# Two small blocks take each half of the weights together, and the first batch's second-half units follow at once

## Chip, cores and metric

One core of a Trainium2 chip runs the kernel. The metric is device microseconds of one execution. The engines are named as in the profile: PE (TensorE matmuls), PEld (its weight loads), DVE (VectorE), ACT (ScalarE), POOL (GpSimd), SP (SyncE, which issues most DMAs).

## What is computed

Attention with a compressed memory for 4 batches of 8 heads of 576 tokens of 64 numbers, then two feed-forward layers over the 2304 tokens of 512 numbers, with 2048 hidden channels. Everything is fp32, and the weights of both layers arrive as 64-bit floats.

```python
scores = scale * np.matmul(q, k.transpose(0, 1, 3, 2))   # causal mask, softmax -> a
local = np.matmul(a, v)
q_p = phi(q)                                             # max(q, 0) + exp(min(q, 0))
mem_out = np.einsum('bhsd,bhde->bhse', q_p, M_prev) / mem_norm
x = g * mem_out + (1 - g) * local
...
h = x @ w_in                                             # layer 1
g = s * np.maximum(h, 0.0) ** 2 + b
x = g @ w_out
...
g = h * np.tanh(sp)                                      # layer 2, sp = log(1 + exp(h))
y = g @ w_out
```

## The kernel before

The order of the work is written by a planner at build time: every step has an engine, a duration, a priority (`prio`, smaller first) and the steps and buffers that it needs. The planner runs through time with these and gives each engine one fixed list. On the chip each engine goes down its list in order and waits at a row until that row's inputs are there.

**Attention.** A unit is two heads of one batch and either the first three tiles of 128 rows (`TA`, called a first-half unit here) or the last two (`TB`, second-half unit). There are 32 units (`pair`, from L429). Each does its score products on PE (L539), row minima on DVE (L549), exponentials on ACT (L557), sums and reciprocals (L504, L578), a scaling of the rows (L573 on ACT, L575 on DVE or POOL), transposes on PE (L598) with copies on ACT (L603), and a product with the values (L620). Its result goes through `xs` (L635) to `x_d` in memory (L637). In the first batch the scaling of a first-half unit is done by DVE, in later batches by POOL; a second-half unit has one tile scaled by ACT and one by DVE.

The inputs of the first four units lie in the weight buffers of the last quarter (`PLACE`, `STAGED`), the following ones in one buffer each of `qk`, `qn` and `vx`; a second one of each comes when the layer-1 weights are all converted. The order of units is: four first-half units of batch 0, then in turn a second-half unit of one batch and a first-half unit of the next. Their priorities are 7 apart (`STEP`).

**Weights of layer 1.** 32 pieces (`convert`) of 128x512 words, in four quarters: of each quarter (`r`) four pieces of `w_in`, then four of `w_out`. Each costs DVE three rows (L685, L687, L697), ACT two (L683, L694) and POOL one (L679). Their raw words pass through `stage` and through weight buffers that are not yet in use.

**Layer 1.** Tokens in three small blocks of 256 and three of 512. A small block goes through the 16 groups of hidden channels in 8 pairs: for each pair 24 matmuls with `w_in` (L780) into the one bank `h`, then `rt` (ACT L829, DVE L835), `gh` and `gl` (ACT L838, DVE L840), then 24 matmuls with `w_out` (L856) that add up in two banks. Two matmuls with zeros (L852) open those banks for a block. A pair's second product comes two pairs after its first (`LAG1`), and `h` is one bank, so the first product of a pair waits for `rt` of the one before it. Block 0 takes the first 256 tokens straight from the attention (`xh`, `xl`, L632, L633); the other blocks load theirs back from `x_d` (`load_x`, L799 to L801). A block needs all four quarters of the weights one after the other. All this has low priority on PE (500 and up), so it fills PE between the steps of the units. Until the first of it, PE's gaps are filled with products of zeros (L1234).

The three large blocks begin when the attention is over; layer 2 follows.

Of the kernel before, what the change touches and what calls it, by code (L numbers as in the profile page):

```python
# [29 lines left out]
STEP = 7.0  # L30
# [7 lines left out]
PLACE = (0, 1, 2, 3)  # L38
STAGED = 4
# [299 lines left out]
def attention_then_two_ffn(ctx: ExitStack, tc: tile.TileContext, qk, qz, vm, beta,  # L339
# [101 lines left out]
    def pair(b, p, prio, g, place=None, apart=False):  # L441
# [14 lines left out]
        if place is None:  # L456
            qk_b, qn_b, vx_b = (Buf(R[x], [P, n]) for x, n in zip(("qk", "qn", "vx"), sizes))
            starts = 0, 0, 0
        else:
            qk_b = qn_b = vx_b = Buf(R[("wih", "wil", "woh", "wol")[place], NR - 1], [P, sum(sizes)])  # L460
            starts = 0, sizes[0], sizes[0] + sizes[1]
# [52 lines left out]
        if apart:  # L514
            low = [Buf(R["Pt3"], [P, 4 * P]) for _ in range(2)]
            high = [Buf(R["Pt4"], [P, 5 * P]) for _ in range(2)]
            Pt = {(i, t): ((low, 0), (high, 0), (high, 2 * P))[t] for t in g for i in range(2)}
            Pt = {(i, t): (x[i], a) for (i, t), (x, a) in Pt.items()}
        else:
            Pt = {(i, t): (Buf(R[f"Pt{t}"], [P, P * (t + 1)]), 0) for t in g for i in range(2)}  # L520
# [106 lines left out]
        k = 0  # L627
# [7 lines left out]
        add(ACT, act_us(m - k) - 0.04, lambda: nc.scalar.copy(xs.t[:, k:m], pv.t[:, skip + k:n]), [pv], [xs])  # L635
        c0 = b * S + q0
        add(DMA, 0.7, lambda: nc.sync.dma_start(x_d[:, p, c0 + k:c0 + m], xs.t[:, k:m]), [xs], [x_in[b, groups_all.index(g)]])  # L637
# [206 lines left out]
    def y_part(j, fcs, acc, t, gh, gl, gh_bufs, gl_bufs, prio):  # L844
# [4 lines left out]
        def y(part, k, fc):  # L849
            if fc == 0 and part == 0 and not big:  # L850
                for a in acc:
                    nc.tensor.matmul(a.t.rearrange("p (k n) -> p k n", n=P), zeros,  # L852
                                     zeros.unsqueeze(1).to_broadcast([P, 4, P]), start=True, stop=False)
            x, nm = ((gh, "woh"), (gh, "wol"), (gl, "woh"))[part]
            for ec in range(NCC):
                nc.tensor.matmul(acc[ec // per].t[:, (ec % per) * n:(ec % per + 1) * n],  # L856
                                 w_at(nm, fc // FPR, fc % FPR)[:, ec * P:(ec + 1) * P], t(x)[:, k * n:(k + 1) * n],
                                 start=(big and fc == 0 and part == 0),
                                 stop=(fc == NFC - 1 and part == 2 and ec % per == per - 1))

        for part in range(3):
            for k, fc in enumerate(fcs):
                need = [*(gl_bufs if part == 2 else gh_bufs), W["wol" if part == 1 else "woh", fc // FPR]]
                add(PE, 0.48 if not big else 0.908, prio, lambda part=part, k=k, fc=fc: y(part, k, fc),
                    need + (acc if fc or part else []), acc, keep=[gh[0]])

    def y_out(j, acc, prio):

        t0, n = blocks1[j]
# [3 lines left out]
        mine = [y_in[t1 // N1] for t1 in range(t0, t0 + n, N1)]  # L873
        for a in (2, 3, 0, 1) if big else (0, 1):
            place = "xr" if not big else "yr" if j < NB1 - 1 else "xh" if a % 2 else "xl"
            ys, act = Buf(R[place], [P, per, n]), a % 2 == 1

            def evacuate(a=a, act=act, ys=ys):
                (nc.scalar.copy if act else nc.vector.tensor_copy)(ys.t, acc[a].t.rearrange("p (k n) -> p k n", n=n))

            add(ACT if act else DVE, 0.7, prio, evacuate, [acc[a]], [ys])
            add(DMA, 0.002 * n * per, prio, lambda a=a, ys=ys: nc.sync.dma_start(
                y_d[:, a * per:(a + 1) * per, t0:t0 + n], ys.t), [ys], mine)
# [225 lines left out]
    halves_ = [(0, p, TA) for p in range(H // 2)]  # L1109
    for i in range(B * H // 2):  # L1110
        halves_.append((*divmod(i, H // 2), TB))
        if i + H // 2 < B * H // 2:
            halves_.append((*divmod(i + H // 2, H // 2), TA))
    for i, x in enumerate(halves_[:STAGED]):
        pair(x[0], x[1], STEP * i, x[2], PLACE[i % len(PLACE)], i < H // 2 and i % 2 == 1)
# [3 lines left out]
    for i, p in enumerate(pieces):  # L1119
        convert(1, 3.0 * i - 1.0 if i < 4 else 22.0 + 2.0 * (i - 4) if i < 8 else 30.0 + 2.4 * (i - 8), *p, raws[i])  # L1120
# [3 lines left out]
    for i, x in enumerate(halves_[STAGED:]):  # L1124
        pair(x[0], x[1], STEP * (i + STAGED), x[2])

# [5 lines left out]
    seq = [(j, tuple(range(fc, fc + 2 - (j >= NB1 - NBIG)))) for j in range(NB1) for fc in range(0, NFC, 2 - (j >= NB1 - NBIG))]  # L1132

    def rank1(j, fc):
        i = NFC * j + fc
        i += max(0, i - NFC * (NB1 - NBIG))
        return RANK1 + i
# [4 lines left out]
    for i in range(len(seq)):  # L1142
        order1.append((i, True))
        for k in range(n, len(seq)):
            if k + LAG1[seq[k][0] >= NB1 - NBIG] > i and i < len(seq) - 1:
# [3 lines left out]
    for i, begins in order1:  # L1149
        j, fcs = seq[i]  # L1150
        little, m0 = j < NB1 - NBIG, len(plan.steps)
        if begins:
            if fcs[0] == 0:
                if j > 0:
                    load_x(j, -1.0)
                accs[j] = [Buf(R[x], [P, 512]) for x in BANKS[j]]
            at_ = rank1(j, fcs[0])
# [125 lines left out]
```

## Time and profile before

| | us |
|---|---|
| median of three timed runs | 986.79 (985.3 to 987.03) |
| the profiled execution | 990.28 |
| its span, first to last instruction | 988.2 |
| PE busy in the span | 956.4 |

The profiled execution is 3.5 us (0.35%) above the median of the timed runs, and 2.1 us of it lie outside the span. PE's busy time counts the products with zeros, 98 before the first layer-1 product. In the profile a row of a group gives line, engine, operation, output and inputs, count, busy time and mean duration, then the idle time before it and what ended that. The rows quoted below are numbered in groups.

### The profile page before, as it was taken

What the parts mean: (1) busy time and instruction counts of PE and PEld (TensorE: products, weight loads), DVE (VectorE), ACT (ScalarE), POOL (GpSimd) and SP (SyncE); (2) the same over time, 40 slices, a digit from 0 to 9 for tenths busy, and PEclk for the clock granted to TensorE, in tenths of its full rate; (3) what the DMA queues carried; (4) which work ended last, traced back from release to release, by engine and by line L of the source; (5) the groups of instructions that cost most, each with busy time, mean ns of one, the idle gap of its engine ahead of it and who ended that gap; (6) DMA issues with size and microseconds to landing.
All of it is one profiled execution on the core that took longest, in us unless ns stands there. A gap on an engine that the chain in (4) does not pass through costs nothing.

```text
span 988.2 us, 18045 instructions
## 1 busy us (share of the span) xinstructions
PE 956.4 (97%) x6304; PEld 850.5 (86%) x6304; DVE 668.6 (68%) x1614; ACT 637.9 (65%) x1377; POOL 191.3 (19%) x354
## 2 busy tenths in 40 slices
PE   6899888999999999999999999999999999999998
PEld 5678577887878898888888888999999999999998
DVE  6989987765765366688612143489966799567864
ACT  4878768777797668798745566366643466344552
POOL 5536656553552000000000000000010001100100
PEclk9989999999999999999999999999999999999999
DMA  9756465544454179998730134487686666676465
GB/s 233 226 182 198 132 185 161 163 116 111 127 137 120 52 237 279 281 315 271 244 115 1 43 128 160 129 269 268 217 298 225 205 206 225 230 242 201 146 218 176
DMA packets 98730, 184.68 MB, mean 187 GB/s; under 512 B 12880, under 2 KB 73296, under 8 KB 91344
## 3 DMA queue, kind: packets, MB, share of 16 engines
q1 hardware_dynamic: 91152, 132.15, 43.2%
q0 software_dynamic: 7056, 51.38, 15.4%
q8 instruction: 50, 0.82, 0.3%
q14 instruction: 40, 0.33, 0.1%
q10 hardware_dynamic: 432, 0.01, 0.0%
HBM read 141.04 MB, written 42.47 MB: 186 GB/s over the span
## 4 chain that ended last, share of the span: by engine, by line
PE 64%; issue 18%; DMA 1%; POOL 1%; DVE 1%; ACT 1%; SPq 0%; POOLq 0%; DVEq 0%
PE bank L856 19%; PE bank L780 18%; PE bank L986 10%; PE bank L1052 7%; PE bank L620 4%; PE bank L598 4%; PE bank L539 3%; DMA woh<-wi_split_d 1%; DMA xr<-x_d 1%; POOL woh L967 1%; POOL wol L967 0%; ACT Pt L557 0%; POOL woh L946 0%; ACT PT L603 0%; DVE stage L685 0%
## 5 line engine op out<-in xcount | busy, mean ns | idle before, releaser
L1052 PE MATMUL bank<-wol,S 128*128 128x256 f32 x828 | 111.6, 283 | 0.0
L1052 PEld LDWEIGHTS bank<-wol,S 128*128 128x128 f32 x828 | 105.3, 192 | 0.0
L967 POOL DMA_DIRECT2D wol<-wo_split_d x17 | 9.2, 540 | 457.9 <-DMA stage<-wo_d 350.7
L986 PE MATMUL bank<-wi,woh 128*128 128x384 f32 x423 | 97.1, 335 | 0.7 <-DMA woh<-wi_split_d 0.7
L557 ACT ACTIVATE Pt<-Pt,mx 128x64 f32<-128x64 f32 (+4 forms) x160 | 88.7, 562 | 8.5 <-DVE mx L549 7.1
L1052 PE MATMUL bank<-woh,S 128*128 128x256 f32 x684 | 93.1, 283 | 0.0
L1052 PEld LDWEIGHTS bank<-woh,S 128*128 128x128 f32 x684 | 87.1, 192 | 0.0
L603 ACT COPY PT<-bank 128x384 f32<-128x384 f32 (+2 forms) x160 | 67.8, 489 | 28.6 <-PE bank L598 25.5
L598 PE MATMUL bank<-ident,Pt 128*128 128x128 f32 x480 | 68.5, 280 | 10.2 <-DVE Pt L575 5.8
L986 PEld LDWEIGHTS bank<-wi,woh 128*128 128x128 f32 x423 | 75.3, 188 | 1.7 <-DMA woh<-wi_split_d 1.1
L560 POOL TENSOR_SCALAR Pt<-ex,nm 128x64 f32<-128x64 f32 x160 | 63.1, 415 | 60.4 <-DVE nm L512 20.9
L549 DVE CUSTOM_DVE_ANT_0 Pt<-bank,mask 128x64 f32<-128x64 f32 (+3 forms) x160 | 54.4, 376 | 27.4 <-PE bank L539 24.3
L986 PE MATMUL bank<-wi,wol 128*128 128x384 f32 x297 | 70.2, 334 | 0.0
L598 PEld LDWEIGHTS bank<-ident,Pt 128*128 128x128 f32 x480 | 55.2, 143 | 14.3 <-POOL stage L679 5.8
L856 PE MATMUL bank<-xh,woh 128*128 128x512 f32 x240 | 64.2, 389 | 0.0
L829 ACT ACTIVATE g<-bank 128x512 f32<-128x512 f32 x48 | 28.7, 597 | 45.9 <-PE bank L780 39.2
L839 DVE TENSOR_TENSOR xh<-g,xh 128x512 fp32r<-128x512 f32 x30 | 20.7, 691 | 49.1 <-ACT xh L837 48.7
L986 PEld LDWEIGHTS bank<-wi,wol 128*128 128x128 f32 x297 | 53.1, 188 | 0.4
L856 PEld LDWEIGHTS bank<-xh,woh 128*128 128x128 f32 x240 | 45.0, 188 | 9.0
L780 PE MATMUL bank<-yh,wi 128*128 128x512 f32 x192 | 51.0, 390 | 0.0
L575 POOL TENSOR_SCALAR Pt<-Pt,rs 128x64 f32<-128x64 f32 (+2 forms) x72 | 38.5, 554 | 49.5 <-DVE rs L578 19.2
L539 PE MATMUL bank<-qk 64*128 64x64 f32 (+4 forms) x228 | 39.2, 465 | 2.8 <-DMA qk<-in_qk 2.3
(257 smaller groups left out, 2338.9 us busy)
## 6 DMA issues: line engine op xcount, KB each, us to landing
wol<-wo_split_d POOLq DMA_DIRECT2D x17, 1024.0 KB, 5.2
woh<-wo_split_d POOLq DMA_DIRECT2D x16, 1024.0 KB, 5.9
wo_split_d<-high SPq DMA_DIRECT2D x44, 256.0 KB, 4.5
stage<-in_w_in SPq DMA_DIRECT2D x21, 512.0 KB, 5.1
woh<-wi_split_d POOLq DMA_DIRECT2D x10, 1024.0 KB, 5.3
stage<-in_w_out SPq DMA_DIRECT2D x19, 512.0 KB, 5.2
stage<-wi_d SPq DMA_DIRECT2D x24, 384.0 KB, 4.6
wi_split_d<-woh SPq DMA_DIRECT2D x8, 1024.0 KB, 4.8
```

Source lines behind the costliest of these rows:

```text
L539: nc.tensor.matmul(ps[k][i].t[:, a:a + hi - lo], qkt(t * P, P)[rows(i)], kt(lo, hi - lo)[rows(i)], start=True, stop=True)
L549: nc.vector.tensor_tensor_reduce(at_t(i, t, D + lo, D + hi), x.t[:, a:a + hi - lo], mask[:, SP - w + lo:SP - w + hi], -SCALE, mx.t[:, i, t ...
L557: nc.scalar.activation(at_t(i, t, D, w + D), at_t(i, t, D, w + D), AF.Exp, bias=mx.t[:, i, t + k:t + k + 1], scale=-1.0, accum_out=rs.t[:, ...
L560: add(POOL, 0.33, lambda i=i, t=t: nc.gpsimd.tensor_scalar(at_t(i, t, 0, D), ex.t[:, i, t - lo_t, :], nm.t[:, i, t - lo_t:t - lo_t + 1], 1 ...
L575: (nc.vector if e == DVE else nc.gpsimd).tensor_scalar(x, x, r, *((None, ALU.mult) if e == DVE else (1.0, ALU.mult, ALU.mult)))
L598: nc.tensor.transpose(ps.t[:, x, :], at_t(i, t, c * P, (c + 1) * P), ident)
L603: (nc.vector.tensor_copy if dve else nc.scalar.copy)(PT[i].t[:, x:x + n], ps.t[:, :n])
L620: nc.tensor.matmul(pv.t[rows(i), cols].rearrange("p (t q) -> p t q", q=P), vx()[:, i, c, :], PT[i].t[:, f[0]:f[-1] + 1:f[1] - f[0] if len( ...
L780: nc.tensor.matmul(ph, w_at(nm, r, cc)[:, o:o + P], x_at(x, cc), start=(begin and part == 0 and cc == 0), stop=(part == 2 and cc == NCC - ...
L856: nc.tensor.matmul(acc[ec // per].t[:, (ec % per) * n:(ec % per + 1) * n], w_at(nm, fc // FPR, fc % FPR)[:, ec * P:(ec + 1) * P], t(x)[:, ...
L986: nc.tensor.matmul(ps.t[:, :H2], w[i // 4].t[:, j, kk, i % 4], x[kk].t[:, k], start=begin and part == kk == 0, stop=part == 2 and kk == 1, ...
L1052: nc.tensor.matmul(acc[t].t[:, :DH], s.t[:, j, t * P:(t + 1) * P], x.t[:, k, q % 4], start=q == part == 0, stop=q == NQ2 - 1 and part == 2)
```

## The change

The first two small blocks (`EARLY`) go through the hidden channels in two parts: block 0 with the first half of the weights (quarters 0 and 1), block 1 with the same, then block 0 with the second half and block 1 with it. Block 2 is as before. Each part opens its two banks with zeros, so there are four more such matmuls. After a part with the first half the sums go to `y_d`; after the second they are read back (DMA into `xr`), added by DVE and stored. `load_x` runs once more for each of the two blocks, so block 0's 256 tokens are now also written to `x_d` (`xs` of 320 columns instead of 64 in four units).

The four second-half units of batch 0 come right after its first-half units, with priorities 28, 33, 38 and 43. Their inputs lie in weight buffers of their own (`woh` and `wol` of quarter 2, `wih` and `wil` of quarter 3), and every other one has its probabilities in `woh` and `wol` of quarter 3, so that two can be under way. After them the remaining 24 units come batch by batch, first half and second half of each pair of heads in turn. The conversions have a table of priorities (`CONV`), one entry for the four pieces of a quarter's `w_in` or `w_out`.

```diff
-STEP = 7.0
+TIME_A, FIRST_B, TIME_B, FIRST, TIME = 7.0, 28.0, 5.0, 50.0, 7.0
+CONV = ((-1.0, 3.0), (24.0, 2.0), (32.0, 2.0), (40.0, 2.0), (50.0, 3.0), (62.0, 3.0), (74.0, 3.0), (86.0, 3.0))
...
-PLACE = (0, 1, 2, 3)
-STAGED = 4
+EARLY = 2
...
-            qk_b = qn_b = vx_b = Buf(R[("wih", "wil", "woh", "wol")[place], NR - 1], [P, sum(sizes)])
+            qk_b = qn_b = vx_b = Buf(R[place], [P, sum(sizes)])
...
-        if apart:
+        if apart and lo_t == 0:
             low = [Buf(R["Pt3"], [P, 4 * P]) for _ in range(2)]
             high = [Buf(R["Pt4"], [P, 5 * P]) for _ in range(2)]
             Pt = {(i, t): ((low, 0), (high, 0), (high, 2 * P))[t] for t in g for i in range(2)}
             Pt = {(i, t): (x[i], a) for (i, t), (x, a) in Pt.items()}
+        elif apart:
+            both = [Buf(R[nm, NR - 1], [P, 9 * P]) for nm in ("woh", "wol")]
+            Pt = {(i, t): (both[i], 4 * P * (t - lo_t)) for t in g for i in range(2)}
         else:
             Pt = {(i, t): (Buf(R[f"Pt{t}"], [P, P * (t + 1)]), 0) for t in g for i in range(2)}
...
-        k = 0
         if b == 0 and lo_t == 0:
...
-        add(ACT, act_us(m - k) - 0.04, lambda: nc.scalar.copy(xs.t[:, k:m], pv.t[:, skip + k:n]), [pv], [xs])
+        add(ACT, act_us(m) - 0.04, lambda: nc.scalar.copy(xs.t[:, :m], pv.t[:, skip:n]), [pv], [xs])
         c0 = b * S + q0
-        add(DMA, 0.7, lambda: nc.sync.dma_start(x_d[:, p, c0 + k:c0 + m], xs.t[:, k:m]), [xs], [x_in[b, groups_all.index(g)]])
+        add(DMA, 0.7, lambda: nc.sync.dma_start(x_d[:, p, c0:c0 + m], xs.t[:, :m]), [xs], [x_in[b, groups_all.index(g)]])
...
-            if fc == 0 and part == 0 and not big:
+            if fc == begin and part == 0 and not big:
...
+    y_partial = {}
+
+    def y_out(part_, acc, prio):
+
+        j, begin, end = part_
         t0, n = blocks1[j]
         per = 512 // n
 
         big = n > N1
-        mine = [y_in[t1 // N1] for t1 in range(t0, t0 + n, N1)]
+        mine = [y_in[t1 // N1] for t1 in range(t0, t0 + n, N1)] if end == NFC else [y_partial.setdefault(j, Buf())]
         for a in (2, 3, 0, 1) if big else (0, 1):
             place = "xr" if not big else "yr" if j < NB1 - 1 else "xh" if a % 2 else "xl"
             ys, act = Buf(R[place], [P, per, n]), a % 2 == 1
 
+            def rows(a=a):
+                return y_d[:, a * per:(a + 1) * per, t0:t0 + n]
+
             def evacuate(a=a, act=act, ys=ys):
-                (nc.scalar.copy if act else nc.vector.tensor_copy)(ys.t, acc[a].t.rearrange("p (k n) -> p k n", n=n))
-
-            add(ACT if act else DVE, 0.7, prio, evacuate, [acc[a]], [ys])
-            add(DMA, 0.002 * n * per, prio, lambda a=a, ys=ys: nc.sync.dma_start(
-                y_d[:, a * per:(a + 1) * per, t0:t0 + n], ys.t), [ys], mine)
+                x = acc[a].t.rearrange("p (k n) -> p k n", n=n)
+                if begin:
+                    nc.vector.tensor_tensor(ys.t, x, ys.t, op=ALU.add)
+                else:
+                    (nc.scalar.copy if act else nc.vector.tensor_copy)(ys.t, x)
+
+            if begin:
+                add(DMA, 0.002 * n * per, prio, lambda ys=ys, rows=rows: nc.sync.dma_start(ys.t, rows()), [y_partial[j]], [ys])
+            add(ACT if act and not begin else DVE, 0.7, prio, evacuate, [acc[a]] + [ys] * (begin > 0), [ys])
+            add(DMA, 0.002 * n * per, prio, lambda ys=ys, rows=rows: nc.sync.dma_start(rows(), ys.t), [ys], mine)
...
-    halves_ = [(0, p, TA) for p in range(H // 2)]
-    for i in range(B * H // 2):
-        halves_.append((*divmod(i, H // 2), TB))
-        if i + H // 2 < B * H // 2:
-            halves_.append((*divmod(i + H // 2, H // 2), TA))
-    for i, x in enumerate(halves_[:STAGED]):
-        pair(x[0], x[1], STEP * i, x[2], PLACE[i % len(PLACE)], i < H // 2 and i % 2 == 1)
+    halves_ = [(0, p, TA, TIME_A * p, (nm, NR - 1), p % 2) for p, nm in enumerate(("wih", "wil", "woh", "wol"))]
+    halves_ += [(0, p, TB, FIRST_B + TIME_B * p, x, p % 2) for p, x in enumerate((("woh", 2), ("wol", 2), ("wih", 3), ("wil", 3)))]
+    halves_ += [(1 + i // H, i % H // 2, (TA, TB)[i % 2], FIRST + TIME * i) for i in range(3 * H)]
+    for b, p, g, prio, *x in halves_[:H]:
+        pair(b, p, prio, g, *x)
     raws = [raw_buf(i // 8, i % 8) for i in range(len(pieces))]
     weight_bufs()
     n = len(plan.steps)
     for i, p in enumerate(pieces):
-        convert(1, 3.0 * i - 1.0 if i < 4 else 22.0 + 2.0 * (i - 4) if i < 8 else 30.0 + 2.4 * (i - 8), *p, raws[i])
+        convert(1, CONV[i // 4][0] + CONV[i // 4][1] * (i % 4), *p, raws[i])
     conversion_left = add(NONE, 0.0, 0.0, lambda: None, after=plan.steps[n:])
     for x, a in zip(("qk", "qn", "vx"), (0, 832, 1344)):
         R[x].homes(stage, [a], conversion_left)
-    for i, x in enumerate(halves_[STAGED:]):
-        pair(x[0], x[1], STEP * (i + STAGED), x[2])
+    for b, p, g, prio in halves_[H:]:
+        pair(b, p, prio, g)
 
     opened = add(NONE, 0.0, 0.0, open_second, after=attention_steps)
     R["h"].banks(banks[1:2], opened)
     rings(m2a, opened, raw=1, yr=4, yh=2, yl=2, g=2)
     for i in range(4):
         R[f"o{i}"] = Ring(f"o{i}").banks(banks[4 + i:5 + i], opened)
-    seq = [(j, tuple(range(fc, fc + 2 - (j >= NB1 - NBIG)))) for j in range(NB1) for fc in range(0, NFC, 2 - (j >= NB1 - NBIG))]
-
-    def rank1(j, fc):
-        i = NFC * j + fc
-        i += max(0, i - NFC * (NB1 - NBIG))
-        return RANK1 + i
+    parts = [(j, lo, lo + NFC // 2) for lo in (0, NFC // 2) for j in range(EARLY)] + [(j, 0, NFC) for j in range(EARLY, NB1)]
+    seq, ranks = [], {}
+    for part in parts:
+        per = 1 + (part[0] < NB1 - NBIG)
+        for fc in range(*part[1:], per):
+            ranks[len(seq)] = RANK1 + sum(len(x) * blocks1[y[0]][1] // N1 for y, x in seq)
+            seq.append((part, tuple(range(fc, fc + per))))
...
```

In the lists below `wi` is the buffer that holds both parts of a quarter of `w_in` (quarters 0 and 1), `wih` and `wil`, `woh` and `wol` are high and low parts; the number behind a name tells buffers apart. Lines of the new kernel are 2 to 14 higher in this place.

PE's list before, where layer 1 begins (about 51 us in the trace): value product of the fourth unit, first pair of block 0, scores of the sixth unit.

```order
L620 MATMUL bank_112<-PT_613,wol_0_159 64x128
L780 MATMUL bank_106<-xh_324,wi_157 128x256 x8
L780 MATMUL bank_106<-xl_333,wi_157 128x256 x4
L780 MATMUL bank_106<-xh_324,wi_157 128x256 x8
L780 MATMUL bank_106<-xl_333,wi_157 128x256 x4
L539 MATMUL bank_110<-qk_659 128x64
L539 MATMUL bank_112<-qk_659 128x64
```

The same place in the new list.

```order
L623 MATMUL bank_112<-PT_620,wol_0_159 64x128
L1248 MATMUL bank_109<-zeros 128x256 x4
L542 MATMUL bank_110<-wol_0_218 128x448
L542 MATMUL bank_113<-wol_0_218 128x448
L542 MATMUL bank_110<-wol_0_218 128x64
L542 MATMUL bank_113<-wol_0_218 128x64
L1248 MATMUL bank_109<-zeros 128x256
L542 MATMUL bank_107<-wol_0_218 128x512
L542 MATMUL bank_111<-wol_0_218 128x512
L782 MATMUL bank_106<-xh_335,wi_157 128x256 x8
```

The sixth unit's scores moved ahead of layer 1's first product, and they read a weight buffer (`wol_0_218`) in place of `qk`.

PE's list before at the ninth first product (about 152 us): the end of block 0's eighth pair, the start of block 1 (`xh_1870`), transposes of the twelfth unit.

```order
L780 MATMUL bank_106<-xh_324,wih_0_1541 128x256 x4
L780 MATMUL bank_106<-xh_324,wil_0_1559 128x256 x4
L780 MATMUL bank_106<-xl_333,wih_0_1541 128x256 x4
L780 MATMUL bank_106<-xh_1870,wi_157 128x256 x8
L598 MATMUL bank_112<-ident,Pt_0_1637 128x128
L598 MATMUL bank_112<-ident,Pt_0_1639 128x128 x2
L780 MATMUL bank_106<-xl_1876,wi_157 128x256 x4
```

The new list at its ninth first product: block 0's second half (`xh_1616`, third quarter of `w_in`), between second products of block 1 (`gl_1797`, `gh_1982`) and transposes of the thirteenth unit.

```order
L859 MATMUL bank_109<-gl_1797,woh_0_1000 128x256 x2
L782 MATMUL bank_106<-xh_1616,wil_0_1356 128x256 x4
L859 MATMUL bank_108<-gh_1982,woh_0_1000 128x256 x2
L859 MATMUL bank_109<-gh_1982,woh_0_1000 128x256 x2
L782 MATMUL bank_106<-xl_1954,wih_0_1342 128x256 x4
L601 MATMUL bank_113<-ident,Pt_0_1762 128x128
L601 MATMUL bank_113<-ident,Pt_0_1764 128x128 x2
```

Where three pairs' first products stood one behind the other, second products of block 1 now stand between them.

DVE's list before, where block 1's tokens are split (`xl_1876`): it stands among the last conversions, those of `w_out`'s last quarter.

```order
L697 TENSOR_TENSOR wol_0_1796<-stage,woh_0_1779 128x512
L685 SCALAR_TENSOR_TENSOR stage<-stage 128x512
L801 TENSOR_TENSOR xl_1876<-xr_1817,xh_1870 128x512
L835 SCALAR_TENSOR_TENSOR rt_1874<-bank_106,rt_1874 128x512
L801 TENSOR_TENSOR xl_1876<-xr_1823,xh_1870 128x512
L687 SCALAR_TENSOR_TENSOR stage<-stage 128x512
```

The same in the new list: it stands among those of `w_in`'s third quarter, and behind it the first sums of block 0 are copied out (`xr_1458`).

```order
L699 TENSOR_TENSOR wil_0_1356<-stage,wih_0_1342 128x512
L803 TENSOR_TENSOR xl_1447<-xr_1375,xh_1436 128x512
L552 ISA Pt_0_1398,mx_1400<-bank_107,mask 128x320
L552 ISA mx_1400 128x1
L803 TENSOR_TENSOR xl_1447<-xr_1381,xh_1436 128x512
L892 COPY xr_1458<-bank_108 128x512
L689 SCALAR_TENSOR_TENSOR stage<-stage 128x512
```

Before, 28 conversions stand ahead of the first of these splits; now it is 19.

## Rows read from the trace of the kernel before

**Rows 1.** Stretches: length, then busy us and count of each engine, clock, DMA.

```profile
48.00:165.00 117.00, 103.20 (x753) 82.62 (x752) 105.31 (x285) 89.43 (x221) 66.33 (x101) 0.94 0.56 170
165.00:345.00 180.00, 180.00 (x1480) 147.17 (x1479) 109.57 (x404) 141.86 (x385) 72.63 (x159) 1.00 0.44 121
345.00:988.00 643.00, 639.22 (x3847) 593.18 (x3845) 416.00 (x799) 375.30 (x682) 26.07 (x49) 1.00 0.62 205
```

**Rows 2.** Waits of PE, 50 to 165 us: us in total, times, longest.

```profile
PE bank L539 <- DMA qk<-in_qk: 2.3, 2, 1.7
...
PE bank L780 <- DVE rt L835: 3.9, 2, 2.4
PE bank L598 <- POOL Pt L575: 2.3, 3, 1.3
PE bank L780 <- ACT wih L694: 1.8, 1, 1.8
```

**Rows 3.** PE in order of time: start, us, row, idle before.

```profile
155.16 1.22 PE L780 MATMUL bank<-xh,wi 128*128 128x256 f32 x8 [2.42 <-DVE rt L835]
...
167.76 2.13 PE L598 MATMUL bank<-ident,Pt 128*128 128x128 f32 x18
```

**Rows 4.** DVE's groups by shape, 50 to 165 us: busy us, mean ns, idle before.

```profile
L685 DVE SCALAR_TENSOR_TENSOR stage<-stage 128x512 int32<-128x512 int32 x14 | 9.9, 715 | 0.5 <-ACT stage L683 0.5
...
L549 DVE CUSTOM_DVE_ANT_0 Pt<-bank,mask,mx 128x512 f32<-128x512 f32 x10 | 7.1, 737 | 0.0
L840 DVE SCALAR_TENSOR_TENSOR gl<-rt,sb,gh 128x512 fp32r<-128x512 f32 x8 | 6.4, 803 | 0.2
L835 DVE SCALAR_TENSOR_TENSOR rt<-bank,rt 128x512 f32<-128x512 f32 x9 | 6.1, 682 | 2.1 <-ACT rt L829 2.1
L549 DVE CUSTOM_DVE_ANT_0 Pt<-bank,mask 128x448 f32<-128x448 f32 x10 | 6.1, 616 | 1.1 <-PE bank L539 1.1
...
L575 DVE TENSOR_SCALAR Pt<-Pt,rs 128x576 f32<-128x576 f32 x8 | 4.2, 572 | 0.0
```

**Rows 5.** DVE in order of time: neighbouring starts, and four places.

```profile
41.12 0.68 DVE L697 TENSOR_TENSOR wol<-stage,woh 128x512 fp32r<-128x512 f32 x1
41.72 0.68 DVE L685 SCALAR_TENSOR_TENSOR stage<-stage 128x512 int32<-128x512 int32 x1
...
56.59 0.66 DVE L835 SCALAR_TENSOR_TENSOR rt<-bank,rt 128x512 f32<-128x512 f32 x1
...
153.75 0.75 DVE L801 TENSOR_TENSOR xl<-xr,xh 128x512 fp32r<-128x512 f32 x1 [0.19 <-ACT xh L800]
154.42 0.68 DVE L835 SCALAR_TENSOR_TENSOR rt<-bank,rt 128x512 f32<-128x512 f32 x1
...
166.13 0.18 DVE L578 RECIPROCAL rs<-rs 128x4 f32<-128x4 f32 x1
```

**Rows 6.** Waits of DVE, 50 to 100 us.

```profile
DVE ex L508 <- ACT ex L507: 1.8, 1, 1.8
...
DVE rt L835 <- ACT rt L829: 1.3, 2, 1.0
DVE wi L697 <- ACT wi L694: 1.3, 1, 1.3
```

**Rows 7.** Scalings on POOL, 164 to 176 us: start, us.

```profile
174.53 1.88 POOL L575 TENSOR_SCALAR Pt<-Pt,rs 128x64 f32<-128x64 f32 x4 [0.96 <-DVE rs L578]
```

**Rows 8.** PE, opening two banks with zeros.

```profile
183.05 0.62 PE L852 MATMUL bank<-zeros 128*128 128x512 f32 x2
```

**Rows 9.** DMA issues to 340 us: count, KB each, median us to landing.

```profile
x_d<-xs SPq DMA_DIRECT2D x15, 128.0 KB, 3.4
...
xr<-x_d SPq DMA_DIRECT2D x4, 256.0 KB, 5.0
```

**Rows 10.** PE late in the attention: unit 28's scores, its first transposes.

```profile
286.99 1.36 PE L539 MATMUL bank<-stage 64*128 64x64 f32 x12
...
298.49 0.49 PE L598 MATMUL bank<-ident,Pt 128*128 128x128 f32 x3
```

More of the change, by code (lines that the diff above doesn't have):

```diff
@@ L842, in first, with y_part @@
         return t, gh, gl, gh_bufs, gl_bufs
-    def y_part(j, fcs, acc, t, gh, gl, gh_bufs, gl_bufs, prio):
+    def y_part(part_, fcs, acc, t, gh, gl, gh_bufs, gl_bufs, prio):
+        j, begin, end = part_
         n = blocks1[j][1]
@@ L857, in y @@
                                  w_at(nm, fc // FPR, fc % FPR)[:, ec * P:(ec + 1) * P], t(x)[:, k * n:(k + 1) * n],
-                                 start=(big and fc == 0 and part == 0),
-                                 stop=(fc == NFC - 1 and part == 2 and ec % per == per - 1))
+                                 start=(big and fc == begin and part == 0),
+                                 stop=(fc == end - 1 and part == 2 and ec % per == per - 1))
         for part in range(3):
@@ L864, in y_part @@
                 add(PE, 0.48 if not big else 0.908, prio, lambda part=part, k=k, fc=fc: y(part, k, fc),
-                    need + (acc if fc or part else []), acc, keep=[gh[0]])
-    def y_out(j, acc, prio):
+                    need + (acc if fc > begin or part else []), acc, keep=[gh[0]])
+    y_partial = {}
+    def y_out(part_, acc, prio):
+        j, begin, end = part_
         t0, n = blocks1[j]
@@ L1144, in attention_then_two_ffn @@
         for k in range(n, len(seq)):
-            if k + LAG1[seq[k][0] >= NB1 - NBIG] > i and i < len(seq) - 1:
+            if k + LAG1[seq[k][0][0] >= NB1 - NBIG] > i and i < len(seq) - 1:
                 break
@@ L1149, in attention_then_two_ffn @@
     for i, begins in order1:
-        j, fcs = seq[i]
+        part, fcs = seq[i]
+        j = part[0]
         little, m0 = j < NB1 - NBIG, len(plan.steps)
         if begins:
-            if fcs[0] == 0:
-                if j > 0:
+            if fcs[0] == part[1]:
+                if i > 0:
                     load_x(j, -1.0)
-                accs[j] = [Buf(R[x], [P, 512]) for x in BANKS[j]]
-            at_ = rank1(j, fcs[0])
+                accs[part] = [Buf(R[x], [P, 512]) for x in BANKS[j]]
+            at_ = ranks[i]
             m = len(plan.steps)
@@ L1161, in attention_then_two_ffn @@
         else:
-            y_part(j, fcs, accs[j], *halves.pop(i), at_ + 0.01)
+            y_part(part, fcs, accs[part], *halves.pop(i), at_ + 0.01)
             out_steps[fcs[0] // FPR] += plan.steps[m0:]
             m = len(plan.steps)
-            if fcs[-1] == NFC - 1:
-                y_out(j, accs[j], -1.0)
+            if fcs[-1] == part[2] - 1:
+                y_out(part, accs[part], -1.0)
         if little:
```

## Prediction, made before the changed kernel ran

> **What bounds the kernel now.** I read the stretches first [rows 1]. From 165 to 345 us, and again to the end, PE is busy without a gap (180.00 of 180.00; then 639.22 of 643.00, the rest being mostly the end). From 48 to 165 us it is busy for 103.2 of 117, and its clock stands at 0.94. So PE's total work sets the end, and time can be won only where PE stands idle or slow ahead of 165 us: 13.8 us of idle time, and 117 x 0.06 = 7.0 us at the lower of the two clock levels, 20.8 us together. Up to about 48 us the two lists are nearly alike, so nothing is taken from there. DVE in the same stretch is busy for 105.3 of 117. PE's waits [rows 2] say who is late: `rt`, scalings of the probabilities, a converted weight, and twice the load of `qk`. Three of the four go back to DVE's list, which carries the conversions of the weights. So I take it that DVE feeds PE up to 165 us, and that this stretch is a race between what DVE has to do ahead of a certain row and what PE has to do ahead of the row that needs it.
>
> From before's row 2041 of PE's work (counted in matmuls, about 343 us) the two lists are the same to the end. A gain made by then stays, since PE has no wait after it [rows 1].
>
> **The ledger.** I count down both lists of DVE, each row at its distance to the next in the trace: a row of 512 words takes 0.60 (41.12 to 41.72 [rows 5]; the mean durations [rows 4] overlap by 0.08 and hold some collisions). A conversion is three of them, 1.8 us. A pair's `rt` and `gl` take 1.3. A second-half unit has minima of 2 x (0.54 + 0.14 + 0.67), a scaling of 2 x 0.43 and some 1.4 of small work, 4.9 in all (the durations less the overlap [rows 4]). A first-half unit counted the same way is 5.1 in the first batch and 3.4 later, where POOL scales. PE's rows are counted likewise at 0.12 for a 256-column matmul of layer 1, and without the products of zeros that fill gaps.
>
> Before, at the transposes of unit 13, DVE has 130 us of work behind it (32 conversions 58, 13 units 59, 9 pairs 11.5, one block's tokens 1.3) and PE 113.4. In the trace these two are at 166.13 and 167.76 [rows 3, 5]. So DVE runs 36 us behind its bare list and PE 54.4 behind its own. At the first `rt` the list has 42 and the trace 56.59 [rows 5]: the lag of 14.6 there grows to 36 by waits and collisions.
>
> After, at the transposes of unit 13, DVE has 125 behind it (27 conversions, 13 units with one second-half unit more, 7 pairs and a half, two blocks' tokens, one copy) and PE 115.8. With before's lag at 125, which I take as 33.8 (32.4 at 122 and 36 at 130, [rows 5]), DVE gets there at 158.8; POOL's first three scalings add 1.4 [rows 7], and the transposes come at 160.2, 44.4 behind PE's bare list. At unit 14 it is 135 for DVE and 126.1 for PE: with a lag kept at 36, and 1.5 for ACT's scaling, 172.5, which is 46.4 behind. At the eleventh first product (145 against 137) it is again 44.7. After that PE has more work behind it than DVE can delay. So PE's lag ends at 46.4 in place of 54.4: **8.0 us** won. It comes from the weights: PE has two blocks of work from the first 16 conversions, and the others are needed later.
>
> **Part by part.** The four more products that open banks cost PE 0.5 a pair [rows 8], 1.0 in all, on the path. What the second parts add on DVE (two more loads of tokens at 1.3, four more rows of sums at 0.6, 5.0 us) and on ACT (about 3) stands in the ledger as far as it lies ahead of unit 14; the rest falls between 165 and 345 us, where DVE has 70 and ACT 38 us free [rows 1]. Reading sums back is two DMAs for each of the two blocks, issued in the list more than ten units of work ahead of their use; I count nothing, and if they came late DVE would stand for up to 5.0 us [rows 9] where it has that spare.
>
> Moving the second-half units: the sixth unit's scores no longer wait for the single `qk` (2.3 us, [rows 2]). Behind that wait DVE lost 1.8, 1.3 and 1.0 on `ex`, `wi` and `rt` [rows 6], of which none has its reason in the new list, while other waits may take their place. The bounds are 0 and 4.1; I take half, 2.0, as one of the two chains behind the wait (ACT's) is as full as before. On SP's list some 2 MB of unit inputs now stand ahead of the conversions of `w_out`'s first quarter. Their first use on DVE is at about 46 us, and I see some 4 us of slack: counted at nothing, up to 3 us if that is gone.
>
> Sum: 8.0 - 1.0 + 2.0 = **9.0 us**. The profiled execution's 990.28 would be 981.3, and the median of 986.79, which lies 3.5 lower, 977.8.
>
> A row on POOL bears on the lag. DVE's conversions take 715 ns on average where 0.60 is their pace [rows 4, 5], and POOL's scalings stand in the same stretch [rows 7]. The Trainium skill (SBUF — State Buffer, section Who interferes with whom) says that a DVE instruction with two inputs in SBUF contends with a GpSimd one that reads SBUF. By that, two units fewer scaled on POOL ahead of unit 13 would take an estimated 1 us off the lag, and the sum would be 10; by the row alone it stays 9.0.
>
> **Rivals.** (1) The stall moves to block 1's tokens. Unit 8's result must go to `x_d` and back ahead of the fifth first product: 3.4 and 5.0 us by median [rows 9]. I have it stored at about 102 us, so ready at 111.5, and the ledger has DVE at the split at 117: 5.5 spare. If the two DMAs take 15 us, or the lag of DVE is that much shorter, ACT and DVE both stand in order behind the load, the lag grows by 4 to 6 us and the gain is **3 to 5**: 982 to 984. Against it: in the trace before, the same way cost DVE a wait of 0.19 [rows 5]. The Trainium skill (DMA: Bandwidth & Descriptors, section Anatomy of one DMA) gives a DMA about 2 us of fixed cost; by that page, as an estimate of 4 us and the bytes for the two, this rival would have nearly no chance. The rows show double that, and I keep it.
>
> (2) No gain. If the lag of DVE is not its own, but ACT's and POOL's waits grow by 8 us as DVE is asked for more units early, unit 14 comes as late as before: **986 to 988**. It decides at a lag of 44 at unit 14 in place of 36. For it: the lag grew by 21.4 over 88 us of list. Carried on at that rate it is 37 at 135, not 44.
>
> (3) Slower, late in the attention. In the new list fewer layer-1 products stand between units after unit 18: the bare PE work from a unit's scores to its transposes is 10.0 to 11.9 us, 11.4 in the mean, where before it is 12 to 13.5 up to unit 27. If a unit needs 12.5 from scores to transposes, PE stands 1.1 at each of 14 units, 15 us, less the 9 won: **+6, 993**. It decides where a unit needs more than 12.05 (9 / 14 above 11.4). Against it: before's own unit 28, where the list has 11.0, did it in 10.1 us (286.99 + 1.36 to 298.49) with no idle time [rows 1, 10].
>
> **How the numbers follow.** A gain of 5 to 14 as worked out has 0.60, rival 1 with a gain of 2 to 5 has 0.14, no gain has 0.11, slower 0.13 (0.10 of it by rival 3), more than 14 has 0.02. The predicted time is 977.8. The best that the terms allow is 10.0 (unit 13 alone decides) - 1.0 + 4.1 = 13.1 and some 1 us of clock, 972.8. Upwards the range takes in rival 1 and half of no gain, up to 987.0; about 0.03 lie below and 0.17 above. A change of 0.2% (2 us) is about what a measurement can tell. Faster by that has 0.76, within it 0.11, slower 0.13.
>
> **What will show it.** Right: PE's last wait ahead of 190 us ends with 45 to 47 us behind its bare list, idle time from 48 to 190 us is 6 to 10, no wait for `qk` at 55 us, fewer stretches of half clock, and no idle time from 190 to 345 us. Rival 1 shows as a wait of ACT for `xr` near 110 us, rival 2 as DVE waits for ACT and POOL of over 15 us up to 165 us, rival 3 as PE waits at L601 after 200 us. The prediction is wrong if PE has 13 us or more of idle time between 48 and 345 us.

## The result, and the profile after

The changed kernel takes 974.45 us (median of 4, 973.69 to 976.78), the kernel before 986.04 beside it (4 runs). The ratio is 0.9888 with a 95% interval of 0.9865 to 0.9912: 11 us faster, where 9.0 were forecast. The profiled executions differ by more, 990.28 to 973.69; before's stood 3.5 above its median and after's stands 0.8 below its own. So before's rows hold some 4 us that a typical execution does not.

The stretches of after, with the columns of [rows 1] (length, then busy us and count of PE, PEld, DVE, ACT and POOL, clock, DMA share, GB/s):

```profile
48.00:165.00 117.00, 110.77 (x880) 89.98 (x878) 110.79 (x307) 103.72 (x248) 63.94 (x97) 1.00 0.63 192
165.00:345.00 180.00, 180.00 (x1483) 149.99 (x1482) 121.47 (x411) 142.82 (x382) 72.55 (x162) 1.00 0.55 158
```

From 48 to 165 us PE's idle time falls from 13.8 to 6.2 us and the clock rises from 0.94 to 1.00, which is 7.0 us of lower clock before and none after. From 165 us on PE is full, as it was. All the waits of PE left in 50 to 165 us, against [rows 2] (total, times, longest):

```profile
PE bank L782 <- ACT xh L802: 1.6, 2, 1.0
PE bank L601 <- ACT woh L576: 1.4, 1, 1.4
PE bank L782 <- DVE rt L837: 1.3, 1, 1.3
PE bank L601 <- ACT Pt L576: 1.0, 1, 1.0
PE bank L601 <- ACT PT L606: 0.9, 1, 0.9
```

The `qk` wait, the wait for a weight and one of two `rt` waits are gone, and block 1's tokens (`xh`) are a new one. DVE's largest waits in 50 to 165 us, against [rows 6]; all of them together are 4.8 us, where before they were 10.8:

```profile
DVE rt L837 <- ACT rt L831: 1.9, 3, 1.1
DVE wil L687 <- ACT wil L685: 1.0, 1, 1.0
DVE stage L689 <- POOL stage L681: 0.9, 1, 0.9
```

In order of time, DVE's last small row of unit 13 and PE's first transposes of it, the two places that the ledger set against each other [rows 3, 5]:

```profile
151.47 0.18 DVE L581 RECIPROCAL rs<-rs 128x6 f32<-128x6 f32 x1
```

```profile
154.25 0.49 PE L601 MATMUL bank<-ident,Pt 128*128 128x128 f32 x3
```

They were forecast at 158.8 and 160.2.

### The profile page after: what moved, and what is told of

Its sections match the earlier page's. It is cut to its first block, busy times and chain, and to the rows that moved or that the text cites. A ratio compares the mean times of both kernels' runs of the same rounds, so it can differ in the third digit from the quotient of the medians.

```text
span 971.9 us, 18071 instructions
## 1 busy us (share of the span) xinstructions
PE 949.1 (98%) x6310; PEld 845.3 (87%) x6310; DVE 672.4 (69%) x1622; ACT 641.1 (66%) x1381; POOL 190.0 (20%) x354
## 4 chain that ended last, share of the span: by engine, by line
PE 84%; issue 6%; DMA 4%; DVE 2%; ACT 1%; POOL 1%; SPq 0%; POOLq 0%; ACTq 0%
PE bank L782 20%; PE bank L859 20%; PE bank L1000 16%; PE bank L1066 13%; PE bank L623 5%; PE bank L601 5%; PE bank L542 5%; DMA wil<-in_w_in 1%; DMA woh<-wi_split_d 1%; DMA woh<-wo_split_d 1%; DMA x_d<-xs 1%; DMA wih<-in_qz 1%; POOL Pt L563 0%; ACT Pt L560 0%; DVE stage L689 0%
## 5 line engine op out<-in xcount | busy, mean ns | idle before, releaser
L560 ACT ACTIVATE Pt<-Pt,mx 128x64 f32<-128x64 f32 (+4 forms) x152 | 83.5, 558 | 10.1 <-DVE mx L552 9.0
L563 POOL TENSOR_SCALAR Pt<-ex,nm 128x64 f32<-128x64 f32 x152 | 58.6, 407 | 59.2 <-DVE nm L512 29.2
L601 PE MATMUL bank<-ident,Pt 128*128 128x128 f32 x444 | 61.8, 276 | 6.6 <-DVE Pt L578 4.5
L552 DVE CUSTOM_DVE_ANT_0 Pt<-bank,mask 128x64 f32<-128x64 f32 (+3 forms) x152 | 50.2, 371 | 17.6 <-PE bank L542 10.9
L601 PEld LDWEIGHTS bank<-ident,Pt 128*128 128x128 f32 x444 | 50.1, 141 | 9.4 <-POOL ex L506 3.7
L782 PEld LDWEIGHTS bank<-yh,wi 128*128 128x128 f32 x192 | 35.5, 188 | 7.0
```

The source lines that it names most:

```text
L552: nc.vector.tensor_tensor_reduce(at_t(i, t, D + lo, D + hi), x.t[:, a:a + hi - lo], mask[:, SP - w + lo:SP - w + hi], -SCALE, mx.t[:, i, t ...
L560: nc.scalar.activation(at_t(i, t, D, w + D), at_t(i, t, D, w + D), AF.Exp, bias=mx.t[:, i, t + k:t + k + 1], scale=-1.0, accum_out=rs.t[:, ...
L563: add(POOL, 0.33, lambda i=i, t=t: nc.gpsimd.tensor_scalar(at_t(i, t, 0, D), ex.t[:, i, t - lo_t, :], nm.t[:, i, t - lo_t:t - lo_t + 1], 1 ...
L601: nc.tensor.transpose(ps.t[:, x, :], at_t(i, t, c * P, (c + 1) * P), ident)
L782: nc.tensor.matmul(ph, w_at(nm, r, cc)[:, o:o + P], x_at(x, cc), start=(begin and part == 0 and cc == 0), stop=(part == 2 and cc == NCC - ...
```

## The experiments

**Theory:** DVE's list feeds PE up to 165 us, and the halves win because PE gets two blocks of work from the first 16 conversions. **Rival A:** the order of the units with two of them under way makes the gain. **Rival B:** the granted clock makes it. All ratios are to the kernel before, run beside on the same chip. "Lost" is PE's idle time from 48 to 165 us plus 117 times what the clock lacks of 1.00, from the row of that stretch. "Block 1" is the start of its first `xh` row on ACT.

| kernel | median | ratio (95% interval) | lost | block 1 |
|---|---|---|---|---|
| before | 986.08 | 1 | 20.8 | 153.1 |
| after | 974.45 | 0.9888 (0.9865 to 0.9912) | 6.2 | 109.7 |
| e1_units_first | 983.18 | 0.9962 (0.9947 to 0.9977) | 13.5 | |
| e2_halves_only | 998.72 | 1.0122 (1.0100 to 1.0143) | 27.9 | 148.9 |
| e3_one_in_flight | 982.25 | 0.9961 (0.9945 to 0.9977) | 13.1 | 114.7 |
| e4_early1 | 988.13 | 1.0012 (0.9993 to 1.0031) | 15.6 | |
| e6_own_inputs | 981.26 | 0.9941 (0.9929 to 0.9953) | 10.2 | 114.3 |
| before_conv_early | 988.10 | 0.9998 (0.9981 to 1.0015) | 16.5 | |
| after_oldconv | 975.07 | 0.9883 (0.9871 to 0.9896) | 6.5 | |
| after_late_conv | 975.12 | 0.9886 (0.9871 to 0.9901) | 7.3 | |
| before_more | 1005.05 | 1.0173 (1.0145 to 1.0201) | 24.3 | |
| after_more | 989.18 | 1.0018 (1.0004 to 1.0032) | 11.6 | |
| before_less | 984.65 | 0.9961 (0.9945 to 0.9977) | 17.7 | |
| after_less | 972.29 | 0.9844 (0.9814 to 0.9873) | 5.8 | |

The kernel before took 986.08 us in the median beside e1 to e4, 987.48 beside the four kernels with a row more or less, and 987.40 beside the rest. Differences in us below are differences of ratios times 986.

### Units alone, halves alone

```diff
-EARLY = 2
+EARLY = 0
```

> The new order of units, their buffers and the new priorities of the conversions stay; no block is split, so block 0 again needs all four quarters of the weights before block 1 begins (EARLY = 0). Theory (the order of the weights makes the gain): at least three quarters of the 11.6 us are gone, 983 us or more, a ratio to the kernel before of 0.997 or more; PE has 12 us or more of idle time between 48 and 165 us, with waits for rt and for weights of the last two quarters. Rival A (the units' order, with no wait for qk and two units under way, makes the gain): 974 to 978 us, ratio 0.988 to 0.992. Rival B (the granted clock makes it): the idle time is as before, and what is won goes with the mean clock of 48 to 165 us, 1.2 us for each 0.01 over 0.94.

Measured: 0.9962, 3.7 us faster than before. The halves are worth the other 7.3. PE's waits from 48 to 345 us, the three largest: layer 1 waits for a weight again, as it did before.

```profile
PE bank L782 <- ACT wih L696: 3.6, 1, 3.6
PE bank L782 <- DVE rt L837: 2.5, 2, 1.9
PE bank L601 <- ACT Pt L576: 1.8, 3, 0.6
```

Two thirds of the gain are gone, where the theory asked for three quarters; PE's idle time from 48 to 165 us is 10.0 us, where it asked for 12 or more. Rival A is out as the whole cause. Then the halves with the units of before (`e2_halves_only`):

```diff
-    for b, p, g, prio, *x in halves_[:H]:
-        pair(b, p, prio, g, *x)
+    # order, staging and priorities of the units as in the kernel before
+    for i in range(B * H // 2): ...
```

> The halves of the weights for blocks 0 and 1 and the priorities of the conversions stay; the units go in the order of the kernel before, 7 apart, second-half units with qk, qn and vx and with their own probability buffers. Theory: most of the gain stays, 976 to 981 us, ratio 0.990 to 0.995: 8.0 less 1.0 were put on the halves and 2.0 on the units; the wait for qk near 55 us is back. Rival A: 983 to 988 us, ratio 0.997 to 1.002.

Measured: 1.0122, 12.0 us slower. Both theories missed. Block 1's tokens 256 to 511 come in part from the second-half units of batch 0, and in before's order the last of those four is the eleventh unit. PE in order of time, the first product of block 1 (start, us, row, idle before):

```profile
149.53 0.50 PE L782 MATMUL bank<-xh,wi 128*128 128x256 f32 x2 [0.88 <-ACT xh L802]
150.24 0.98 PE L782 MATMUL bank<-xh,wi 128*128 128x256 f32 x6 [0.20 <-ACT xh L802]
```

The fourth first product had begun at 81.6 us, so PE had none to start for 68 us, and the list holds block 0's second half behind block 1's first. The stretch of 48 to 165 us shows what that cost:

```profile
48.00:165.00 117.00, 97.30 (x686) 71.87 (x683) 105.44 (x298) 94.31 (x239) 74.56 (x112) 0.93 0.66 190
```

So the two parts are worth -3.7 and +12.0 alone and -11.0 together: early second-half units, in buffers of their own, are what the halves stand on. The next two runs tell the place from the buffers.

### What of the units: inputs, or two under way

```diff
-    halves_ += [(0, p, TB, FIRST_B + TIME_B * p, x, p % 2) for p, x in ...]
+    halves_ += [(0, p, TB, FIRST_B + TIME_B * p) for p in range(H // 2)]
```

> As the changed kernel, but the four second-half units of batch 0 take their inputs through qk, qn and vx, one at a time, and ordinary probability buffers; their place in the order stays. Theory: 975 to 979 us, ratio 0.989 to 0.993: a wait for qk of 1 to 3 us and DVE waits behind it come back, nothing else. Rival A (two in flight makes the gain): 981 us or more, ratio 0.995 or more, with DVE waits of over 9 us between 50 and 165 us where the changed kernel has 4.8.

Measured: 0.9961, 7.2 us of the gain lost, in rival A's range of times and outside the theory's. DVE's waits are 7.6 us, though, not over 9 as rival A asked. PE meets block 1's tokens late, and the clock falls behind that wait (PE in order of time, then three stretches):

```profile
115.40 1.10 PE L782 MATMUL bank<-xh,wi 128*128 128x256 f32 x4 [3.63 <-ACT xh L802]
```

```profile
110.00:116.90 6.90, 2.76 (x18) 1.64 (x19) 6.90 (x22) 6.90 (x17) 4.01 (x4) 1.00 0.96 261
116.90:120.30 3.40, 3.40 (x18) 3.39 (x17) 3.40 (x7) 3.22 (x8) 0.82 (x1) 0.50 0.46 154
120.30:125.00 4.70, 4.70 (x38) 2.93 (x38) 4.70 (x13) 2.97 (x9) 2.33 (x5) 1.00 0.48 138
```

Of the 23.1 us between e2 and after, the early place in the order is worth 15.9 (e2 against e3) and the buffers 7.2. The next run keeps the inputs in their own buffers and takes back the second set of probabilities alone:

```diff
-    halves_ += [(0, p, TB, FIRST_B + TIME_B * p, x, p % 2) for p, x in ...]
+    halves_ += [(0, p, TB, FIRST_B + TIME_B * p, x) for p, x in ...]
```

> The changed kernel, but the four second-half units of batch 0 use the ordinary probability buffers; their inputs still lie in weight buffers of their own. It divides the 7.8 us that were lost when both were taken back. If the inputs (no wait for qk, loads issued early) are what counts: 974 to 977 us. If the second set of probabilities (two units under way) is: 980 to 983 us. The price of 2.0 us put on the vanished qk wait says 976 to 978 for the loss of the other part.

Measured: 0.9941. The second set of probabilities, two units under way, is worth 5.2 us (its interval and after's don't overlap), the inputs some 2.0 (0.9961 against 0.9941, the intervals overlap). In the trace the waits of PE for scaled probabilities grow from after's 2.4 (1.4 and 1.0 above) to 5.5:

```profile
PE bank L601 <- ACT Pt L576: 5.5, 3, 2.2
PE bank L782 <- DVE rt L837: 2.4, 2, 1.8
```

The last second-half unit of batch 0 ends 3.4 us later (103.7 against 100.3), and block 1's tokens 4.6 later.

### One block split

```diff
-EARLY = 2
+EARLY = 1
```

> As the changed kernel, but block 0 alone is split (EARLY = 1): its second half follows its first at once, as if it were whole, with the sums stored, read back and added. Block 1's first half no longer stands between. Theory: the gain is gone as in the kernel with no block split, and within 2 us of that one; what it lies above that one is the price of one more pair of opened banks and of the sums read back (estimate 0.5 us from 0.62 us for a pair). Rival (the split as such helps, since sums are copied out earlier or banks come free): 974 to 979 us, ratio 0.988 to 0.993.

Measured: 1.0012. The gain is gone, as the theory says, but the kernel is 4.9 us slower than with no split, where under 2 were expected. PE has three waits for `wih` (4.9 us in all) and three for `rt` (4.1), where e1 has one and two. I did not find what makes them, and the price of splitting a block is left open.

### Is it DVE's list?

The row that merges the sign, twice in each conversion of layer 1, in before and in after:

```diff
+        for _ in range(2 if layer == 1 else 1):
             add(DVE, 0.6, prio, lambda: nc.vector.scalar_tensor_tensor(...), ...)
```

> The kernel before, with DVE's row that merges the sign (L685) done twice in each of the 32 conversions of layer 1: 32 x 0.60 = 19.2 us more on DVE up to 165 us, and nothing on other engines. Theory (DVE's list feeds PE up to 165 us): 14 to 20 us slower than the kernel before, 1000 to 1006 us, ratio 1.014 to 1.021, since all 32 stand ahead of the transposes of unit 13. Rival (the units' own chain through ACT and POOL sets the pace, and DVE's waits of 10.8 us swallow the rows): 0 to 8 us slower.

> The changed kernel with the same 32 rows twice. Theory: 27 conversions stand ahead of unit 13, so 16.2 us at most, and 11 to 16 us slower than the changed kernel: 985 to 991 us, ratio to the kernel before 0.999 to 1.005; the change is then worth more (13 to 16 us) than with single rows. Rival (the gain was the mutual waits of the engines, which are gone): DVE has spare time now and the rows cost under 8 us, 982 us or less.

Measured: 17.1 us slower in before and 12.8 in after, both in the theory's ranges. The change is worth 15.3 us here. Part of this lies ahead of the stretch that was meant: the first product of layer 1 starts at 55.52 us in `before_more` (before 51.56) and at 55.80 in `after_more` (after 53.79), 4.0 and 2.0 us later. Then the row left out (`range(0 if layer == 1 else 1)`):

> The kernel before without that row in the conversions of layer 1, which leaves out the sign of the low words of its weights: 19.2 us less on DVE. Theory: PE's 13.8 us of idle time and 7.0 us of lower clock between 48 and 165 us shrink by two thirds, 968 to 976 us, ratio 0.982 to 0.990. Rival (DVE isn't what is late): 982 us or more.

> The changed kernel without that row, which leaves out the same part: up to 16.2 us less on DVE ahead of unit 13, but only 6.2 us of idle time are left between 48 and 165 us. Theory: 4 to 9 us faster than the changed kernel, 965 to 971 us, ratio 0.979 to 0.985, so that the change is worth 2 to 8 us here, less than with the row. Rival (the gain doesn't hang on DVE): the change is worth the same 11 to 12 us with and without the row.

Measured: only 3.8 us faster in before, and 4.3 in after. The change is worth 11.5 us, as much as with the row. The theory missed on before, and in both runs the rival holds; after's 4.3 lies at the low end of the theory's 4 to 9 as well. In the trace of `before_less`, the stretch and DVE's largest waits from 50 to 165 us:

```profile
48.00:165.00 117.00, 104.01 (x769) 83.21 (x769) 92.97 (x271) 94.40 (x238) 61.86 (x106) 0.96 0.57 171
```

```profile
DVE Pt L549 <- PE bank L539: 6.4, 5, 3.6
DVE rt L836 <- ACT rt L830: 4.4, 3, 2.3
DVE ex L508 <- ACT ex L507: 3.7, 3, 2.0
DVE wi L698 <- ACT wi L695: 2.6, 1, 2.6
DVE gl L841 <- ACT gh L839: 2.6, 4, 1.3
```

DVE's busy time falls by 12.3 against [rows 1] and PE's rises by 0.8. DVE's waits grow from 10.8 to 22.6 us. It now waits for PE's scores and for ACT, which wait for others in turn. The small gain was made ahead of this stretch, as far as the traces tell. PE's first product of layer 1, in before, `before_less`, after and `after_less`:

```profile
51.56 1.41 PE L780 MATMUL bank<-xh,wi 128*128 128x256 f32 x8
47.34 1.11 PE L781 MATMUL bank<-xh,wi 128*128 128x256 f32 x8
53.79 1.22 PE L782 MATMUL bank<-xh,wi 128*128 128x256 f32 x8
49.26 1.22 PE L783 MATMUL bank<-xh,wi 128*128 128x256 f32 x8
```

It comes 4.2 and 4.5 us earlier without the row, as much as was won (3.8 and 4.3). In the stretch, PE's idle time is 13.0 us against 13.8 in before, and 5.8 against 6.2 in after; the clock of 0.96 against 0.94 is no gain of the row, since `before_conv_early` has 0.97 at before's time. The stretch of `after_less`:

```profile
48.00:165.00 117.00, 111.24 (x890) 90.27 (x887) 100.42 (x290) 106.28 (x261) 60.65 (x99) 1.00 0.64 194
```

So DVE is at its limit (more work there costs most of itself) without being the only one. Part of what stands just behind it may be the unit under way, worth 5.2 us in the runs above; whether ACT or the one bank `h` holds the rest, no run here tells. In all four runs the planner wrote the lists anew, so each tests the row together with the lists made for it.

### The place of the conversions

In before, the last 24 pieces were pulled ahead:

```diff
-        convert(1, ... else 30.0 + 2.4 * (i - 8), *p, raws[i])
+        convert(1, ... else 30.0 + 1.6 * (i - 8), *p, raws[i])
```

> The kernel before, with the conversions of the last 24 pieces 1.6 apart in priority in place of 2.4, so that w_in's last quarter stands two units earlier in the lists; no work is added or removed. In the kernel before, the sixth first product of layer 1 starts at 117.2 us and the seventh at 145.0, where that quarter is done (142.6). Theory A (DVE has no time to give up there): the quarter comes some 10 us earlier and the units as much later, the idle time of PE moves to the units' transposes, and the time is within 3 us of the kernel before. Theory B (the place of the conversions behind the units is what makes PE lack products; DVE's waits leave room): seventh first product at 135 us or earlier, 4 to 9 us faster.

Measured: 0.9998, theory A. The seventh first product comes at 130.4 us (before 145.0), the eighth to eleventh units end 3.0, 8.2, 4.6 and 8.2 us later, and PE waits for probabilities (48 to 345 us: total, times, longest):

```profile
PE bank L598 <- ACT Pt L573: 4.5, 3, 4.1
PE bank L598 <- ACT PT L603: 2.2, 4, 1.3
```

In after, the new table was taken back, and in another run spread wider:

```diff
-        convert(1, CONV[i // 4][0] + CONV[i // 4][1] * (i % 4), *p, raws[i])
+        convert(1, 3.0 * i - 1.0 if i < 4 else 22.0 + 2.0 * (i - 4) if i < 8 else 30.0 + 2.4 * (i - 8), *p, raws[i])
```

> The changed kernel with the priorities of the conversions of the kernel before (22 and 2.0 apart, then 30 and 2.4 apart): the last two quarters stand earlier, ahead of units 9 to 14. By the ledger 27 conversions stand ahead of unit 13 with the new table and 32 with this one, 5 x 1.8 = 9 us of DVE's work: 6 to 9 us slower than the changed kernel if DVE's list decides, 980 to 984 us; under 3 us slower if it does not.

```diff
-CONV = (..., (50.0, 3.0), (62.0, 3.0), (74.0, 3.0), (86.0, 3.0))
+CONV = (..., (52.0, 4.0), (68.0, 5.0), (84.0, 5.0), (104.0, 5.0))
```

> The changed kernel, with the conversions of the last two quarters spread wider in priority (52, 68, 84 and 104, 4 to 5 apart, in place of 50, 62, 74 and 86, 3 apart): w_in's last quarter is done at 151.6 us there and first used at 174.8, so there are 23 us to give to the units. If the waits of PE for units (3.3 us of the 6.2 of idle time between 48 and 165 us) are due to conversions ahead of them: 1 to 3 us faster than the changed kernel, 971 to 974 us. If the conversions are then late for block 0's second half: idle time at 150 to 200 us, 976 us or more.

Measured: 0.9883 and 0.9886, the same as after. The table is worth nothing that shows: neither the 6 to 9 us for DVE's list in the first run nor the 1 to 3 us in the second came. In `after_oldconv` PE reaches unit 13 like this:

```profile
164.71 0.49 PE L601 MATMUL bank<-ident,Pt 128*128 128x128 f32 x3
164.96 0.72 PE L859 MATMUL bank<-gl,woh 128*128 128x256 f32 x4
```

That is 10.5 us later than in after, and yet no time is lost. Ahead of that row PE has done 10 first and 8.7 second products in place of 8.5 and 7.2, which is 3 x 24 matmuls at 0.12, 8.6 us. Of conversions 29 stand ahead of it there, not the 32 that I had assumed (27 in after). The planner had exchanged one sort of work for another on both engines. No version here beats after by more than the intervals, `after_less` included.

## Why the prediction was right

**What bounds the kernel** held: the gain came from 48 to 165 us alone, and nothing was lost behind it. The table's "lost" follows the times: against after, e1 lost 7.3 more and is 7.3 slower, e2 21.7 and 23.1, e3 6.9 and 7.2, e4 9.4 and 12.2, e6 4.0 and 5.2. It does not for the row done twice: `before_more` lost 3.5 more than before and is 17.1 slower. There the first product comes 4.0 later, PE loses 5 us more from 165 to 345 us (3.3 idle, the rest clock), and before's own profile stands some 4 us high.

**The 8.0 less 1.0** of the halves measured 7.3 (e1 against after). The direction of the ledger held: PE has two blocks of work from the first 16 conversions. Its detail did not. At unit 13 DVE was 151.5 - 125 = 26.5 behind its list, where I kept 33.8 from before, and PE was 154.25 - 115.8 = 38.4 behind its own, where I had 44.4; PE's last wait ended at 130.15, so the sign of 45 to 47 failed, while the other signs (6.2 us of idle time, no `qk` wait, no half clock, no idle time behind) came. Some 4 us of this may be before's own profiled execution, which the ledger took as typical: `before_conv_early`, equal in time, lost 16.5 where before's row has 20.8.

The sum was wrong too: 27 conversions, one second-half unit in place of a first-half one, seven and a half pairs, the tokens of two blocks and one copy come to some 122 by my own prices, not 125. The rows that stand ahead of the two places in the traces, each less 0.08, come to 139.8 us before and 131.8 after, 8 less and not 5. (Ahead of block 1's first split the trace has 30 conversions in before, where I counted 28; after's 19 are right.) With 2.6 us less on DVE the gain at unit 14 is 10.6, and 9.6 after the cost of the banks. So it is luck that 7.0 and the measured 7.3 lie so close.

More weighty: a ledger at one row, with DVE's lag carried over as DVE's own, says when that row comes but not what the change is worth. `after_oldconv` moved that row by 10.5 us for nothing, and `before_less` took 12.3 us off DVE in the stretch for nothing that shows there.

**The 2.0** of the units was the mis-sized term: 3.7 alone (e1). I put it on the vanished `qk` wait and the waits behind it. The runs put about 2.0 on the inputs, and 5.2 on two units under way, for which the sum had no term. The two terms are not independent either: alone the halves lose 12.0, so what a part "measures" depends on what stands beside it. With the right sum of the ledger the forecast would have been 11.6, as near to the 11.0, but with 2.3 too much on the halves and 1.7 too little on the units. That the total is better than its parts is luck too.

**The clock** had no term but 1 us in the range, and 7.0 us of lower clock in before's rows went to none. In `before_conv_early`, with the same time, it is 3.5. Rival B is not the main cause: between after and e3 only 1.2 of 6.9 lost us are clock. The timed runs say the same. Over whole executions before has a mean clock of 0.993 in the median, after 0.997; the two executions of before that had 0.997 took 984.3 and 984.6 us, against after's 974.45. So at the same clock some 10 us are left, and by the step of 0.004 (4 us of 986) at least 7. The falls follow PE's waits, as in e3 above and in before:

```profile
150.00:156.60 6.60, 4.17 (x35) 3.97 (x35) 6.16 (x14) 5.80 (x14) 5.34 (x7) 1.00 0.57 187
156.60:160.00 3.40, 3.40 (x18) 3.40 (x18) 3.40 (x6) 2.10 (x5) 2.31 (x3) 0.50 0.00 0
```

**Rival 1** came in small. The tokens were split from 109.7 us on, when I had DVE there at 117, so the 5.5 us spare were gone (the tokens had been put at 111.5, though 102 + 3.4 + 5.0 is 110.4); PE waited twice, 1.6 us in all:

```profile
110.38 0.50 PE L782 MATMUL bank<-xh,wi 128*128 128x256 f32 x2 [0.58 <-ACT xh L802]
111.88 0.39 PE L782 MATMUL bank<-xh,wi 128*128 128x256 f32 x1 [0.99 <-ACT xh L802]
```

Unit 8's `xs` row starts at 100.35 and the two loads into `xr` landed 4.3 and 5.6 us after their issue, more than the estimate of 2.6 that the Trainium skill (DMA: Bandwidth & Descriptors, section Anatomy of one DMA) would give for 256 KB; the page tells it of DMAs that GpSimd issues, and these are SP's. The measurement decides. **Rival 2** fell: DVE's waits went down to 4.8, not above 15. **Rival 3** fell: PE is busy for 180.00 of 180.00.

**POOL's rows.** One group of DVE's conversion rows takes 728 ns in the mean in after, against 715 in [rows 4], though fewer units are scaled on POOL ahead of unit 13:

```profile
L687 DVE SCALAR_TENSOR_TENSOR stage<-stage 128x512 int32<-128x512 int32 x13 | 9.4, 728 | 0.1
```

All conversion rows from 50 to 165 us together go the other way, 712 ns in after and 729 in before. For 81 rows that is 1.3 us, near the estimated 1 us by the Trainium skill (SBUF — State Buffer, section Who interferes with whom). But `after_oldconv` and e4, with the same order of units, have 723 and 766, so one profile of each kernel doesn't show that the change made the difference. The contention that the prediction quoted agrees with the trace of before: conversion rows that ran beside a row of POOL took 759 ns in the mean (43 rows), the others 685 (30).

## What to carry to other kernels

Before pricing a reordering, ask which work it makes ready early and on what that hangs: here half the weights for two blocks paid because the units that feed the second block came early (with the old order they lost), and more so with two units under way. Here a busy share of 90% said that added work costs, not that removed work pays; test both signs before an engine is called the bound, and look where in the trace the time was won. Where a planner rewrites all lists, don't price a change by one row: compare what each engine has done ahead of it.

## What the runs showed of the hardware

The falls of the clock came in stretches of 3.4 us, or twice that, at 0.50; in every kernel here, each that began between 50 and 200 us stood beside or up to 2.8 us behind waits of PE of 0.9 us or more, and `after_less` had none up to 350 us. Not every wait brought one: after's of 1.3 at 130 us and e3's of 2.4 at 56 us did not. A store and a load through memory took 9.4 us from the start of the `xs` row (100.35) to the split (109.72), 0.4 of it the row itself.
